# Which queue stores the last gradients of the caches: SyncE in place of GpSimd for the final 14 stores, two of them cut in 120 and 8 rows

## The chip, the core and the metric

The kernel runs on one core of a Trainium2 chip. The metric is device time in microseconds, the median of several executions; the profile shows one execution, with its own span. Engines are called TensorE (PE), VectorE (DVE), ScalarE (ACT), GpSimd (POOL) and SyncE (SP). SyncE does no arithmetic here; it issues transfers.

## What is computed

One decode step of a transformer block and its gradients. Forward: layer norm, attention of one query per batch entry over a cache of 4096 keys, output projection, residual, layer norm, a two-layer ReLU network, residual. There are 2 batch entries and 32 heads, so 64 pairs (b, h), each with a key tile and a value tile of 4096 x 128 in bf16 (1 MB). Cut to what matters:

```
q      = layernorm(x) @ wq                       # per head 128 wide
p      = softmax(q k^T / sqrt(128))              # 4096 weights per (b, h)
o      = p v ;  h = x + o @ wo ;  out_0 = h + mlp(layernorm(h))
given grad_out, go = gradient of o:
gV     = p   (outer) go                          # 4096 x 128, out_3
dp     = v go^T ;  gs = p * (dp - p.dp) / sqrt(128)
gK     = gs  (outer) q                           # 4096 x 128, out_2
```

and the gradients of x, wq, wo, w1 and w2. What has to be moved is large beside what has to be computed: all keys once, the values nearly twice (they don't stay on the chip until the gradient is known), and 128 MB of gK and gV back.

## The kernel before

**Two passes.** The first pass (`p1_iter`, index i) loads the K and V tile of a pair, computes scores, softmax and output. The second (`p2_iter`, index j, one call per turn, 64 turns) needs the gradient go of the pair; it takes the value tile Wt (kept from the first pass for 11 pairs, loaded again for 53), transposes it on TensorE in four groups (`pair_transpose`, line 439), multiplies with go (`pair_matvec`, line 452) to get dp, and makes the two outer products. `outer_half` (line 834) makes half of one on VectorE, so four such instructions per turn. gV of turn j is made in turn j; gK of turn j is made at the start of the call for turn j+1, since it needs all of dp. GpSimd copies p into a doubled form pp for gV (line 863).

**Order.** The order of every engine's instructions is written out by hand: the generators of both passes are advanced in turn, and between their steps small jobs from background lists are put in (`bg`, `bg2`, `bg3`: the network in the middle, the weight gradients in `fin_gen`, the gradient of x in `gx_gen`). Each engine then works through its list in that order, and waits where data or buffers aren't there.

**Buffers.** Tiles of 1 MB come from a set of 21 buffers that `take` and `give` hand round, first given first taken, with a tag for each use: "ld" for loads, "g" for gK and gV, "f" for weight gradients, "q" for rows of wq. `share` sets how many of each there are. In the last third of the second pass these are 6, 7, 3 and 5. A buffer given back after a store can be written again only when the store has landed, which the framework enforces with a semaphore.

**Loads.** `queue` is a plain list, filled before the kernel's main loop with all loads of K, V, W and most weights in order. `pump`, called between the steps, issues from its head as long as a buffer "ld" is free, always on SyncE (`load_tile`, line 460). The list is walked while the program is being written out, so that it is empty is known at each store then. Rows of wq for the gradient of x are loaded apart from it (line 980).

**Stores.** gK (line 872) and gV (line 891) are issued from GpSimd. Weight gradients are issued from ScalarE (line 946). The small rows, out_0 and the gradient of x, go through `store_row`, which transposes a column of 5 x 128 values, copies it and stores it from SyncE (line 655). The store of a cache gradient has 128 partitions with 8 KB each:

```
def natural(cache, b, h):
    return cache[b, h].rearrange("(p sc) d -> p sc d", sc=NSC)
```

Of the kernel before, what the change touches and what calls it, by code (L numbers as in the profile page):

```python
# [15 lines left out]
def kernel(  # L16
# [20 lines left out]
    nc = tc.nc  # L37
# [35 lines left out]
    def pst(shape, dtype, role, name):  # L73

        k = banks[role].pop(0)
        banks[role].append(k)
        return ps.tile(shape, dtype, tag=f"bank{k}", bufs=1, name=name)
# [11 lines left out]
    def take(tag, shape, name):  # L89
        assert free[tag] > 0, (tag, name)  # L90
        free[tag] -= 1
        k = homes[tag].pop(0)
        t = pools[k].tile(shape, BF16, tag=f"big{k}", bufs=1, name=name)
        home_of[id(t)] = (tag, k, t)
        return t
# [9 lines left out]
    def give(t, to=None):  # L105
        tag, k, _ = home_of.pop(id(t))
        to = to or goes_to(tag)
        owned[tag] -= 1
        owned[to] += 1
        free[to] += 1  # L110
        homes[to].append(k)
        given_at[k] = step[0]
# [280 lines left out]
    NP1 = len(pairs)  # L393
# [37 lines left out]
    def pair_transpose(nat, g, dve=False, busy=0):  # L431


        t_ps = pst([128, GT // 2, 128], FP32, "tps", "t_ps")
        warm(t_ps[:].rearrange("p j k -> p (j k)"), nat, g, busy)
        natf = nat[:].bitcast(FP32)
        for j in range(GT // 2):
            cc = (g * GT) // 2 + j
            nc.tensor.transpose(t_ps[:, j, :], natf[:, 2 * cc:2 * cc + 2, :].rearrange("p c k -> p (c k)"), ident_f[:])  # L439
        t_sb = mats.tile([128, GT // 2, 128], FP32, tag="XT", bufs=5, name="t_sb")  # L440
        if dve:
            nc.vector.tensor_copy(out=t_sb[:], in_=t_ps[:])
        else:
            nc.scalar.copy(out=t_sb[:], in_=t_ps[:])  # L444
        return t_sb

    def pair_matvec(dst, t_sb, g, vecs):
        v = t_sb[:].bitcast(BF16).rearrange("p j (k two) -> p j k two", two=2)
        for j in range(GT // 2):
            sc = g * GT + 2 * j  # L450
            for par in range(2):
                nc.tensor.matmul(dst[:, sc:sc + 2], lhsT=v[:, j, :, par], rhs=vecs[:, par, :],  # L452
                                 start=(par == 0), stop=(par == 1))

    def natural(cache, b, h):
        return cache[b, h].rearrange("(p sc) d -> p sc d", sc=NSC)
# [192 lines left out]
    def store_row(col_bf, n, dst):  # L649

        t = pst([16, 128], BF16, "mid", "row_ps")
        nc.tensor.transpose(t[0:n, :], col_bf, ident_bf[:])
        r = small.tile([16, 128], BF16, tag="orow", bufs=2, name="orow")
        nc.vector.tensor_copy(out=r[0:n, :], in_=t[0:n, :])
        nc.sync.dma_start(out=dst, in_=r[0:n, :])

    def ttr(in0, in1, acc, width, kc=128, junk=None):
        if junk is None:
# [48 lines left out]
    def mlp_out():  # L707

        ml32 = small.tile([128, ND, B], FP32, tag="ml32", bufs=1, name="ml32")
        nc.vector.memset(ml32[:], 0.0)  # L710
        for k in range(NW2):
            while free["q"] < 1:
                yield
            t = load_w2(k, "q", "(p c) d -> p c d")
            yield from wait(12)
            c1 = min(NF, (k + 1) * FP)
            m_ps = pst([128, ND, B], FP32, "mid", "mlp_ps")
            for c in range(ND):
                for cf in range(k * FP, c1):
                    kc = f_kc(cf)  # L720
                    nc.tensor.matmul(m_ps[:, c, :], lhsT=t[0:kc, cf - k * FP, c * 128:(c + 1) * 128],
                                     rhs=arow[0:kc, cf, :], start=(cf == k * FP), stop=(cf == c1 - 1))
            give(t)
            yield
            nc.vector.tensor_tensor(out=ml32[:], in0=m_ps[:], in1=ml32[:], op=ALU.add)
        ml_bf = small.tile([128, ND, B], BF16, tag="ml_bf", bufs=1, name="ml_bf")
        nc.vector.tensor_copy(out=ml_bf[:], in_=ml32[:])
        y_bf = small.tile([128, B, ND], BF16, tag="y_bf", bufs=1, name="y_bf")
        nc.vector.tensor_tensor(out=y_bf[:].rearrange("p b c -> p c b"), in0=h1c[:], in1=ml_bf[:], op=ALU.add)
        yield from wait(3)  # L730
        for b in range(B):
            store_row(y_bf[:, b, :], ND, out_0[b].rearrange("s (c p) -> (s c) p", p=128))
            yield
# [98 lines left out]
    def outer_half(dst, row, colp, k):  # L832
        sl = slice(k * HALF, (k + 1) * HALF)
        nc.vector.tensor_tensor(  # L834
            out=pairs_view(dst[:, sl, :]),
            in0=row.rearrange("p (a two) -> p a two", two=2)[:, None, :, :].to_broadcast([128, HALF, 64, 2]),
            in1=colp[:, sl, None, :].to_broadcast([128, HALF, 64, 2]), op=ALU.mult)

    def p2_iter(j, busy):

        c = S2[j] if j < NP1 else None
        p = S2[j - 1] if j >= 1 else None
        if p is not None:
            bp, hp = turns[j - 1]
            pair_matvec(p["dp"], p.pop("T3"), 3, gom[:, hp, bp, :, :])
            gsp = small.tile([128, NSC, 2], BF16, tag="gsp", name="gsp")
            nc.vector.scalar_tensor_tensor(
                out=gsp[:], in0=p["dp"][:, :, None].to_broadcast([128, NSC, 2]), scalar=negdot[:, hp, bp:bp + 1],
                in1=P_bf[:, bp * H + hp, :, None].to_broadcast([128, NSC, 2]), op0=ALU.add, op1=ALU.mult)
        if c is not None:  # L850
            b, h = turns[j]
            go = gom[:, h, b, :, :]

            bank = pst([128, 512], FP32, "sps", "dp_ps")
            for k, col in enumerate((goc, qsc)):
                nc.tensor.matmul(bank[:, 128 + k * 128:256 + k * 128],  # L856
                                 lhsT=col[:, h, b:b + 1].to_broadcast([128, 128]), rhs=ident_bf[:],
                                 start=True, stop=True)
            c["dp"] = bank[:, 0:NSC]
            rb = mats.tile([128, 256], BF16, tag="rb", bufs=4, name="rb")  # L860
            nc.scalar.activation(out=rb[:], in_=bank[:, 128:384], func=ACT.Copy, scale=rt[:, b, h:h + 1])  # L861
            pp = small.tile([128, NSC, 2], BF16, tag="pp", name="pp")
            nc.gpsimd.tensor_copy(out=pp[:], in_=P_bf[:, b * H + h, :, None].to_broadcast([128, NSC, 2]))
            c.update(rb=rb, pp=pp)
            c["T0"] = pair_transpose(c["W"], 0, busy=busy)
        if p is not None:
            gK = take("g", [128, NSC, 128], "gK")
            outer_half(gK, p["rb"][:, 128:256], gsp, 0)
        yield
        if p is not None:  # L870
            outer_half(gK, p["rb"][:, 128:256], gsp, 1)
            nc.gpsimd.dma_start(out=natural(out_2, bp, hp), in_=gK[:])  # L872
            give(gK)
            del S2[j - 1]
        yield
        if c is None:
            return
        c["T1"] = pair_transpose(c["W"], 1, busy=busy)
        pair_matvec(c["dp"], c.pop("T0"), 0, go)
        yield  # L880
        c["T2"] = pair_transpose(c["W"], 2, busy=busy)
        pair_matvec(c["dp"], c.pop("T1"), 1, go)
        yield
        c["T3"] = pair_transpose(c["W"], 3, busy=busy)
        give(c["W"], "g" if j < H and j != 1 and owned["g"] < 3 else None)
        pair_matvec(c["dp"], c.pop("T2"), 2, go)
        gV = take("g", [128, NSC, 128], "gV")
        outer_half(gV, c["rb"][:, 0:128], c["pp"], 0)
        yield
        outer_half(gV, c["rb"][:, 0:128], c["pp"], 1)  # L890
        nc.gpsimd.dma_start(out=natural(out_3, b, h), in_=gV[:])  # L891
        give(gV)
        yield

# [79 lines left out]
    def gx_gen(fin):  # L974
# [47 lines left out]
        for b in range(B):  # L1022
            gxo = small.tile([128, ND], BF16, tag="gxo", bufs=2, name="gxo")
            nc.vector.tensor_copy(out=gxo[:], in_=gx_bf[:, :, b])
            yield from wait(2)
            store_row(gxo[:], ND, out_1[b].rearrange("s (c p) -> (s c) p", p=128))
            yield
# [55 lines left out]
    queue = []  # L1083
# [51 lines left out]
    for n, (i, j) in enumerate(plan):  # L1135
# [21 lines left out]
        if j is not None:  # L1157
            while g2 is not None:
                p2_step()
            if j < NP1:  # L1160
                bg_until(("go", *turns[j]))
            g2 = p2_iter(j, 0)
# [93 lines left out]
```

## Time and profile before

| | before |
|---|---|
| median of 3 runs | 910.61 us (910.49 to 913.68) |
| span of the profiled execution | 912.4 us |
| moved by DMA | 363.00 MB, mean 398 GB/s |
| read from and written to HBM | 212.16 MB and 149.13 MB |
| SyncE's queue (all loads, small rows) | 212.18 MB, 58.0% of 16 engines' span |
| GpSimd's queue (gK and gV) | 134.23 MB, 35.5% |
| ScalarE's queue (weight gradients) | 14.91 MB, 4.1% |
| median time from issue to landing, gV and gK | 15.1 and 15.3 us |
| last product of VectorE ends | 896.05 us |

The page gives the busy share of each engine over the whole span, then rows of 40 digits, one for each fortieth of the span, in which 9 means at least 90 per cent. A line of the timeline has the start, the length, the engine, the line of the kernel, the operation, what it writes and reads, and in brackets how long the engine was idle before and what ended that. A line of the windows has for each engine its busy time and number of instructions, then the clock that TensorE was granted, the share of the 16 DMA engines in use, and GB/s. The time from issue to landing counts until the slowest of the 16 engines has reported. A transfer is made of packets, here mostly of 8 KB, one for each partition; the trace has a record of each, with its queue, start and length, though not the number of its DMA engine.

### The profile page before, as it was taken

The page shows a single profiled execution, that of the slowest core. Times are in us where ns is not written, and L with a number is a line of the kernel's source. Part 1 is how long each engine was busy: PE and PEld are TensorE (multiplying, and loading weights), DVE is VectorE, ACT ScalarE, POOL GpSimd, SP SyncE. Part 2 cuts the span into 40 slices and gives each one's busy share as a digit, 9 for nine tenths or more (in the row PEclk, how much of TensorE's full clock was granted, in tenths as well). Part 3 has the DMA queues.
Part 4 walks back from the last instruction along what each step waited for, and adds up shares of the span by engine and source line. Part 5 has one row for each costly group of instructions (what it writes and reads, how often), then busy time and mean ns, then how long its engine had stood idle before and what let it go on. Part 6 is the DMA issues. An engine that isn't in the chain of part 4 may idle for free.

```text
span 912.4 us, 26504 instructions
## 1 busy us (share of the span) xinstructions
PE 739.9 (81%) x11226; PEld 619.8 (68%) x11226; DVE 693.5 (76%) x1291; ACT 530.5 (58%) x1096; POOL 174.2 (19%) x329
## 2 busy tenths in 40 slices
PE   5998899999989898897867844866799778949780
PEld 5887787888878787787757734755667566735460
DVE  4655677877779887786868798977797468999882
ACT  4565455567677776675743433644577656537650
POOL 1222223323201111010011111111232111111120
PEclk9999899999999999998995785766557555555655
DMA  9999999999789999999999999999999999999995
GB/s 346 416 396 411 405 393 410 412 418 375 296 315 334 413 422 421 421 424 418 420 400 391 414 425 412 395 402 389 390 403 390 425 424 426 423 424 424 421 421 247
DMA packets 59479, 363.00 MB, mean 398 GB/s; under 512 B 5697, under 2 KB 15553, under 8 KB 19169
## 3 DMA queue, kind: packets, MB, share of 16 engines
q1 hardware_dynamic: 37920, 212.18, 58.0%
q0 software_dynamic: 18432, 134.23, 35.5%
q10 hardware_dynamic: 3008, 14.91, 4.1%
q8 instruction: 88, 1.44, 0.6%
q14 instruction: 31, 0.25, 0.1%
HBM read 212.16 MB, written 149.13 MB: 396 GB/s over the span
## 4 chain that ended last, share of the span: by engine, by line
PE 38%; DMA 26%; DVE 18%; ACT 10%; issue 6%; POOL 1%; SPq 0%; POOLq 0%; ACTq 0%; DVEq 0%
DMA Vt<-in_A_v_cache_dram 12%; PE t_ps L439 8%; PE m_ps L473 8%; PE t_ps L418 7%; DMA out_dram<-gV 6%; DVE gV L834 5%; DMA out_dram<-gK 5%; ACT t_sb L423 4%; DVE gK L834 3%; PE s_ps L429 3%; ACT t_sb L444 3%; DMA wqs<-in_A_wq_dram 3%; DVE pk L480 3%; DVE junk L660 2%; PE u_ps L502 2%
## 5 line engine op out<-in xcount | busy, mean ns | idle before, releaser
L423 ACT COPY t_sb<-t_ps 128x1024 bf16<-128x1024 bf16 x223 | 217.4, 1017 | 45.1 <-PE t_ps L418 44.8
L444 ACT COPY t_sb<-t_ps 128x512 f32<-128x512 f32 x256 | 149.7, 588 | 131.7 <-PE t_ps L439 128.5
L480 DVE TENSOR_TENSOR pk<-Kt,ep 128x2048 bf16<-128x2048 bf16 x128 | 156.2, 1221 | 55.8 <-ACT ep L528 25.6
L439 PE MATMUL t_ps<-ident_f,Wt 128*128 128x128 f32 x848 | 190.7, 370 | 2.1 <-ACT t_sb L423 2.1
L473 PE MATMUL m_ps<-pk,Vt 128*128 128x129 bf16 x2048 | 172.0, 222 | 16.2 <-DMA Vt<-in_A_v_cache_dram 14.8
L834 DVE TENSOR_TENSOR gK<-rb,gsp 128x2048 bf16<-128x2048 bf16 x128 | 152.5, 1225 | 29.1 <-DMA out_dram<-gV 27.1
L834 DVE TENSOR_TENSOR gV<-rb,pp 128x2048 bf16<-128x2048 bf16 x128 | 152.9, 1218 | 18.4 <-DMA out_dram<-gK 16.3
L418 PE MATMUL t_ps<-ident_bf,Kt 128*128 128x128 bf16 x2048 | 153.1, 224 | 8.6 <-DMA Kt<-in_A_k_cache_dram 3.4
L473 PEld LDWEIGHTS <-Vt 128*128 128x128 bf16 x2048 | 125.4, 99 | 46.7 <-issue 30.0
L439 PEld LDWEIGHTS t_ps<-ident_f,Wt 128*128 128x128 f32 x848 | 131.6, 192 | 35.9 <-issue 28.1
L418 PEld LDWEIGHTS <-Kt 128*128 128x128 bf16 x2048 | 125.6, 100 | 16.2 <-issue 9.1
L452 PEld LDWEIGHTS <-t_sb 128*128 128x128 bf16 x2048 | 95.5, 106 | 44.2 <-issue 18.9
L490 POOL COPY pk<-ep 128x16 bf16<-128x16 bf16 x80 | 66.4, 833 | 189.0 <-ACT ep L528 154.5
L452 PE MATMUL dp_ps<-gom,t_sb 128*128 128x2 bf16 x2048 | 95.0, 167 | 8.9 <-ACT t_sb L444 7.8
L429 PE MATMUL s_ps<-qc,t_sb 128*128 128x1 bf16 x2048 | 88.0, 164 | 1.6 <-DVE t_sb L421 0.8
L891 POOL DMA_DIRECT2D out_dram<-gV x64 | 34.3, 535 | 272.0 <-DVE gV L834 195.0
L872 POOL DMA_DIRECT2D out_dram<-gK x64 | 34.1, 533 | 260.5 <-DVE gK L834 202.0
L429 PEld LDWEIGHTS <-t_sb 128*128 128x128 bf16 x2048 | 77.6, 97 | 4.2 <-ACT t_sb L423 1.2
L944 ACT CAST ot<-o_ps 128x512 bf16<-128x512 f32 (+4 forms) x160 | 70.2, 489 | 17.3 <-DMA out_dram<-ot 11.5
L861 ACT ACTIVATE rb<-dp_ps,rt 128x256 bf16<-128x256 f32 x64 | 30.4, 475 | 60.2 <-PE dp_ps L856 58.9
L587 ACT CAST MT<-m_ps 128x128 bf16<-128x128 f32 x64 | 17.1, 267 | 75.0 <-PE m_ps L473 74.9
L660 DVE CUSTOM_DVE_ANT_0 junk<-wo_t,hbc 128x640 bf16<-128x640 bf16 x64 | 52.3, 817 | 0.2
(194 smaller groups left out, 777.9 us busy)
## 6 DMA issues: line engine op xcount, KB each, us to landing
Kt<-in_A_k_cache_dram SPq DMA_DIRECT2D x64, 1024.0 KB, 14.7
Vt<-in_A_v_cache_dram SPq DMA_DIRECT2D x64, 1024.0 KB, 15.7
out_dram<-gV POOLq DMA_DIRECT2D x64, 1024.0 KB, 15.1
out_dram<-gK POOLq DMA_DIRECT2D x64, 1024.0 KB, 15.3
Wt<-in_A_v_cache_dram SPq DMA_DIRECT2D x53, 1024.0 KB, 12.0
wo_t<-in_A_wo_dram SPq DMA_DIRECT2D x4, 1280.0 KB, 19.4
wqs<-in_A_wq_dram SPq DMA_DIRECT2D x5, 1024.0 KB, 19.8
wq_t<-in_A_wq_dram SPq DMA_DIRECT2D x5, 960.0 KB, 14.7
```

Source lines behind the costliest of these rows:

```text
L418: nc.tensor.transpose(t_ps[:, j, :], nat[:, g * GT + j, :], ident_bf[:])
L423: nc.scalar.copy(out=t_sb[:], in_=t_ps[:])
L429: nc.tensor.matmul(dst[:, sc:sc + 1], lhsT=t_sb[:, j, :], rhs=vec, start=True, stop=True)
L439: nc.tensor.transpose(t_ps[:, j, :], natf[:, 2 * cc:2 * cc + 2, :].rearrange("p c k -> p (c k)"), ident_f[:])
L444: nc.scalar.copy(out=t_sb[:], in_=t_ps[:])
L452: nc.tensor.matmul(dst[:, sc:sc + 2], lhsT=v[:, j, :, par], rhs=vecs[:, par, :], start=(par == 0), stop=(par == 1))
L473: nc.tensor.matmul(r["m"][:, 0:129], lhsT=r["V"][:, sc, :], rhs=r["pk"][sc // HALF][:, sc % HALF, 0:129], start=(sc == 0), stop=(sc == NSC ...
L480: nc.vector.tensor_tensor(out=p["pk"][k][:, :, 0:128].rearrange("p s (a two) -> p s a two", two=2), in0=p["K"][:, sl, :].rearrange("p s (a ...
L490: nc.gpsimd.tensor_copy(out=col, in_=e)
L660: nc.vector.tensor_tensor_reduce(out=junk[0:kc, 0:width], in0=in0, in1=in1, scale=1.0, scalar=0.0, op0=ALU.mult, op1=ALU.add, accum_out=acc)
L834: nc.vector.tensor_tensor(out=pairs_view(dst[:, sl, :]), in0=row.rearrange("p (a two) -> p a two", two=2)[:, None, :, :].to_broadcast([128 ...
L944: nc.scalar.copy(out=ot[0:P, k, n0:n0 + nn], in_=o_ps[0:P, 0:nn])
```

## The change

While loads are still to be issued, gK and gV are stored from GpSimd as before. Once the list of loads is empty, SyncE has nothing to issue, and its queue takes the stores of gK and gV. Two of the last three stores of gK (turns 61 and 62) are cut in two transfers, of the first 120 partitions and of the last 8. The purpose is to use the queue that has become free, and to spread the last transfers otherwise over the DMA engines. The stores of small rows leave SyncE's queue for GpSimd's, so that they don't stand between loads and stores there. What is computed is the same.

```
     def store_row(col_bf, n, dst):
...
-        nc.sync.dma_start(out=dst, in_=r[0:n, :])
+        nc.gpsimd.dma_start(out=dst, in_=r[0:n, :])
...
+    def store_tile(dst, t, uneven=False):
+
+        eng = nc.gpsimd if queue else nc.sync
+        if uneven:
+            eng.dma_start(out=dst[0:120], in_=t[0:120])
+            eng.dma_start(out=dst[120:128], in_=t[120:128])
+        else:
+            eng.dma_start(out=dst, in_=t[:])
...
-            nc.gpsimd.dma_start(out=natural(out_2, bp, hp), in_=gK[:])
+            store_tile(natural(out_2, bp, hp), gK, NP1 - 3 <= j - 1 < NP1 - 1)
...
-        nc.gpsimd.dma_start(out=natural(out_3, b, h), in_=gV[:])
+        store_tile(natural(out_3, b, h), gV)
```

## The prediction

> **What bounds the kernel now.** I read the page first. Turn j is one (b, h) of the second pass; V57 is the store of gV of turn 57, K57 that of gK. From the page:
>
> ```profile
> PE 739.9 (81%) x11226; PEld 619.8 (68%) x11226; DVE 693.5 (76%) x1291; ACT 530.5 (58%) x1096; POOL 174.2 (19%) x329
> DMA  9999999999789999999999999999999999999995
> out_dram<-gV POOLq DMA_DIRECT2D x64, 1024.0 KB, 15.1
> out_dram<-gK POOLq DMA_DIRECT2D x64, 1024.0 KB, 15.3
> ```
>
> No engine is full, but the DMA row is: the transfers bound the kernel up to its last slice, where the digit falls to 5. The change acts there, so next I cut the end into windows (last columns: clock, DMA share, GB/s).
>
> ```profile
> 898.00:900.00 2.00, 0.00 (x0) 0.00 (x0) 0.00 (x0) 0.00 (x0) 0.00 (x0) 0.50 1.02 426
> 901.00:902.00 1.00, 0.00 (x0) 0.00 (x0) 0.00 (x0) 0.00 (x0) 0.00 (x0) 0.50 0.76 320
> 902.00:904.00 2.00, 0.00 (x0) 0.00 (x0) 0.00 (x0) 0.00 (x0) 0.00 (x0) 0.50 0.37 156
> 904.00:906.00 2.00, 0.00 (x0) 0.00 (x0) 0.00 (x0) 0.00 (x0) 0.00 (x0) 0.50 0.17 74
> 908.00:910.00 2.00, 0.00 (x0) 0.00 (x0) 0.00 (x0) 0.00 (x0) 0.00 (x0) 0.50 0.07 29
> ```
>
> All compute is over at 896, and the share is full until 901. Then it falls to 0.17 (under three of 16 engines) and 0.07 (one). So one DMA engine works alone from about 906 to 910. The packet records agree: 11 engines end between 901.2 and 902.7, two at 904.0, then 905.7, 906.1, and one at 910.26. That laggard is never idle at the end: it takes a row of 8 KB each 0.306 us, eight to a store, 2.45 us, and the last stores land 2.45 us apart (905.81, 908.24, 910.66). The span ends 1.73 us after the last landing.
>
> The third view is VectorE's timeline before that:
>
> ```profile
> 854.06 1.22 DVE L834 TENSOR_TENSOR gK<-rb,gsp 128x2048 bf16<-128x2048 bf16 x1 [2.78 <-DMA out_dram<-gV]
> 858.88 1.23 DVE L834 TENSOR_TENSOR gV<-rb,pp 128x2048 bf16<-128x2048 bf16 x1 [0.17 <-DMA out_dram<-gK]
> 877.02 0.28 DVE L847 SCALAR_TENSOR_TENSOR gsp<-dp_ps,negdot,P_bf 128x64 bf16<-128x64 f32 x1 [2.04 <-PE dp_ps L452]
> 893.69 2.36 DVE L834 TENSOR_TENSOR gK<-rb,gsp 128x2048 bf16<-128x2048 bf16 x2
> ```
>
> gV and gK rotate through seven buffers here (share gives g=5+2), so an outer product waits for the landing seven stores earlier: K57 at 854.06 waits for V54, issued 823.01, landed 853.97. These waits total 3 us and are nearly absent later, but with little to spare (below). Last, GpSimd's queue:
>
> ```profile
> 893.75 0.53 POOL L891 DMA_DIRECT2D out_dram<-gV  x1 [1.92 <-DVE gsp L847]
> 896.34 0.53 POOL L872 DMA_DIRECT2D out_dram<-gK  x1 [2.06 <-DVE gK L834]
> ```
>
> K63 is computed by 896.05, issued 0.29 us later, and the earliest engine takes its first row at 898.25, 1.9 us after issue.
>
> [...]from 843 to 857 a busy engine takes in turn one row of GpSimd's queue, one of SyncE's, one (4 KB) of ScalarE's. [...]The two x loads of 10 rows show 10 packets each[...]; the records don't number engines. [...]Here it is 0.96 us (x load issued 0.75, first packet 1.71) against 1.9. The laggard takes none of the five packets of the second 5-row store[...].
>
> **Which stores move.** The list empties when turn 63's Wt load is issued. Six buffers hold Wt, so that load follows turn 57's last transposes, between the halves of gV. In the trace it is issued at 846.10, V57 at 850.25. From V57 on all moves: 7 gV and 7 gK, 14 of 128; K61 and K62 in two parts, so 16 issues on SyncE.
>
> **Part 1, the split.** [...]16 x 0.306 = 4.9 us.[...] Alone, a gain of 3.6 to 4.2 us.
>
> **Part 2, shorter issue.** Issue after VectorE: 0.03 us for SyncE's small store against 0.29. Start: 0.96 against 1.9. Together K63's first row can come 1.2 us earlier after compute. Today this is worth nothing on the laggard, which has 10 us queued when K63 is issued; it counts only if compute sets the end. Behind the waiting stores on SyncE nothing is queued: no load is left (last wqs load 815.08). On GpSimd pp no longer stands behind a store's wait; VectorE is not waiting for pp there, so nothing.
>
> **Part 3, the small rows.** Four stores of 1.2 KB move to GpSimd, 0.53 us each, in idle time. Behind them wait pp copies, of 0.25 to 0.41 us; also nothing. Taking the first two off SyncE frees a Wt load from a wait of at most 4.5 us, in a saturated stretch: nothing.
>
> **Part 4, two queues in place of one.** This is the cost. At 857.2 the last Wt row has passed and GpSimd's queue holds K54 (nearly done), V55, K55, V56, K56. They land now at 858.76, 861.30, 864.31, 868.18, 871.39, with V57 behind them. After the change SyncE's queue has V57 (and K57, V58, ...) ready, and they go row for row with the old ones. Each old store is stretched by up to its own 2.45 us:
>
> K54 +1.0, lands 859.8. V55 +3.5, 864.8. K55 +6.0, 870.3. V56 +8.4, 876.6. K56 +10.9, 882.3.
>
> The newer ones get ahead, but VectorE needs the buffers in the old order. K58 (now 863.76) needs V55: +1.0. V59 (866.57) needs K55: +3.7. K59 (870.26) needs V56: +6.3. V60 (872.54) needs K56: +9.8. From K60 on the needed stores are all SyncE's and long landed. So VectorE is 9.8 us late at V60; the bounds are 8 (SyncE's queue runs dry at times) and 12 (the waits feed back into V57's neighbours, another queue takes turns). It regains its later waits for TensorE (2.04 + 0.69 + 0.36 = 3.1 us), since TensorE can work up to two banks ahead meanwhile. K63 is then computed 6.7 us late, at 902.8 (bounds 901 to 905).
>
> **The sum.** Queues are by then nearly empty, so K63 lands 0.03 + 0.96 + 2.45 + 0.45 (last row to landing, as now) = 3.9 us later: 906.7, or 904.9 to 908.9. The laggard's own limit, if relieved, is 905.4 + 0.45; the second engine's 906.5 to 907.1. The later counts: 906.5 to 908.9, against 910.66. The gain is 1.8 to 4.2 us; I take 2.8, towards the late side of the wait, as part of the 9.8 feeds back. 910.6 - 2.8 = 907.8.
>
> **Rivals.** (A) The old stores aren't held up (the queues are served by age, or buffers are free sooner): only the balance counts, gain 4.2, or 5 if the second engine also catches up: 905.6 to 906.4. For: waits are nearly absent today. Against: strict alternation in the packets. (B) The laggard isn't relieved[...]: its work is unchanged or 0.6 us more: 910.6 to 911.2. For: no numbers in the records. (C) Slower: the delay reaches 12 to 15 us and TensorE gives nothing back, at a clock of 0.5: K63 computed at 908 to 911, landed at 912 to 915, total 911.9 to 915.5. For: every buffer waits on the slowest of 16 engines. Against: while VectorE waits, SyncE's queue drains and the old stores get the whole engine.
>
> **How the numbers follow.** Main case 0.50, A 0.23, B 0.17, C 0.10. The range 905.4 to 911.8 leaves out most of C and a little of A. Half a per cent is 4.55 us: faster needs under 906.06, which is most of A and a sliver of the main case, 0.22. Slower needs over 915.2, the end of C with some unknown: 0.07. Same: 0.71.
>
> **What would show it.** Timeline of VectorE, 860 to 885: several idle times ended by the landing of a store, about 10 us in all, where before there are none; without them A is right. Windows after 900: the share falls without a lone engine of 4 us; if 0.07 stands for 4 us again, B. K63's product ending near 903 and its landing 4 us later show the sum. 57 stores of each kind left on GpSimd. What would make it wrong: a different engine lagging after the change, or the wait for buffers moving to earlier turns.

## The result, and the profile after

| | before | after |
|---|---|---|
| median | 911.67 us (910.49 to 913.68, 4 runs) | 919.58 us (918.83 to 921.13, 4 runs) |
| ratio | | 1.0087, 95% interval 1.0062 to 1.0112 |
| span of the profiled execution | 912.4 us | 916.8 us |
| last product of VectorE ends | 896.05 us | 903.48 us |
| last packet of a store ends | 910.26 us | 915.1 us |

The kernel became slower by about 0.9%. The prediction, 907.8 us with a range up to 911.8, missed on the side to which it had given 7 in 100. The medians lie 7.9 us apart, the two profiled executions only 4.4 us in span (the profiled one of before took 914.32 us, longer than its four timed runs; that of after, 918.83 us, is the shortest of its four). What is read from the profiles below bears on the 4.4 us; the rest isn't traced. From the page of the kernel after, the DMA row, the row of GB/s, and the three groups of stores that take the place of the two shown of before:

```profile
DMA  9999999999889999999999999999999999999987
GB/s 346 419 394 411 407 395 409 413 418 368 310 287 349 421 422 423 422 422 422 411 410 388 408 425 413 398 408 391 392 404 386 425 424 424 421 425 422 424 338 244
out_dram<-gV POOLq DMA_DIRECT2D x57, 1024.0 KB, 13.3
out_dram<-gK POOLq DMA_DIRECT2D x57, 1024.0 KB, 13.8
out_dram<-gV SPq DMA_DIRECT2D x7, 1024.0 KB, 10.7
```

57 stores of each kind stay on GpSimd, as counted. Read the last two columns of the first two rows together. The last but one slice is 80 to 89% busy and moves 338 GB/s; a slice with 9 moves 424. The last digit is higher than before (7 against 5), which on its own would look like the better balance that the change is for.

The windows of the kernel after, in stretches of 2 us (last three columns: clock, DMA share, GB/s):

```profile
892.00:894.00 2.00, 2.00 (x21) 1.88 (x19) 2.00 (x4) 1.17 (x2) 1.08 (x2) 0.50 1.07 439
896.00:898.00 2.00, 2.00 (x17) 1.72 (x16) 1.97 (x4) 1.23 (x3) 0.13 (x1) 0.50 0.94 254
898.00:900.00 2.00, 1.56 (x23) 1.36 (x21) 2.00 (x3) 1.11 (x2) 0.00 (x0) 0.75 1.06 262
902.00:904.00 2.00, 0.00 (x0) 0.00 (x0) 1.48 (x2) 0.00 (x0) 0.00 (x0) 0.61 0.96 307
908.00:910.00 2.00, 0.00 (x0) 0.00 (x0) 0.00 (x0) 0.00 (x0) 0.00 (x0) 0.50 0.97 385
912.00:914.00 2.00, 0.00 (x0) 0.00 (x0) 0.00 (x0) 0.00 (x0) 0.00 (x0) 0.50 0.09 37
```

This is the reading of the case. From 898 to 900 before, a share of 1.02 moved 426 GB/s. Now a share of 1.06 moves 262. The engines are as busy and move 0.6 of the bytes, so the rows take longer. The packet records give it: up to 894.6 nearly all rows of 8 KB take 0.31 us; from 894.64, when the first 120-row part begins to be moved, rows of about 0.6 us appear, and in the 4 us from 896 the mean is 0.507 us.

VectorE's timeline after shows the waits for buffers, and the last product:

```profile
859.60 1.23 DVE L834 TENSOR_TENSOR gV<-rb,pp 128x2048 bf16<-128x2048 bf16 x1 [1.32 <-DMA out_dram<-gK]
871.17 2.36 DVE L834 TENSOR_TENSOR gV<-rb,pp 128x2048 bf16<-128x2048 bf16 x2 [3.58 <-DMA out_dram<-gK]
877.38 2.36 DVE L834 TENSOR_TENSOR gK<-rb,gsp 128x2048 bf16<-128x2048 bf16 x2 [2.57 <-DMA out_dram<-gV]
883.57 2.36 DVE L834 TENSOR_TENSOR gV<-rb,pp 128x2048 bf16<-128x2048 bf16 x2 [3.82 <-DMA out_dram<-gK]
901.12 2.36 DVE L834 TENSOR_TENSOR gK<-rb,gsp 128x2048 bf16<-128x2048 bf16 x2
```

The line at 883.57 is V60, 11.0 us late; in the kernel before it has no wait:

```profile
872.54 2.35 DVE L834 TENSOR_TENSOR gV<-rb,pp 128x2048 bf16<-128x2048 bf16 x2
```

And SyncE's instructions, where line 843 issues a part of 120 rows, 844 one of 8 rows, and 846 a whole store:

```profile
893.78 0.35 SPq L843 DMA_DIRECT2D out_dram<-gK  x1
894.19 0.31 SPq L844 DMA_DIRECT2D out_dram<-gK  x1
896.05 0.36 SPq L846 DMA_DIRECT2D out_dram<-gV  x1
898.64 0.38 SPq L843 DMA_DIRECT2D out_dram<-gK  x1
899.07 1.60 SPq L844 DMA_DIRECT2D out_dram<-gK  x1
900.91 2.63 SPq L846 DMA_DIRECT2D out_dram<-gV  x1
903.64 2.06 SPq L846 DMA_DIRECT2D out_dram<-gK  x1
```

K61's large part takes 7.1 us to land, then V62 9.3, K62's large part 11.5 and V63 12.1 us. The time to landing grows with each of them.

### The profile page after: what moved, and what is told of

The parts are those of the page before. It is cut to its first block, busy times and chain, and to the rows that moved or that the text cites. A ratio compares the mean times of both kernels' runs of the same rounds, so it can differ in the third digit from the quotient of the medians.

```text
span 916.8 us, 26507 instructions
## 1 busy us (share of the span) xinstructions
PE 747.8 (82%) x11226; PEld 626.5 (68%) x11226; DVE 693.5 (76%) x1291; ACT 531.0 (58%) x1096; POOL 169.0 (18%) x319
## 4 chain that ended last, share of the span: by engine, by line
PE 39%; DMA 26%; DVE 19%; ACT 9%; issue 6%; DVEq 0%; SPq 0%; POOL 0%; ACTq 0%; POOLq 0%
DMA Vt<-in_A_v_cache_dram 12%; PE t_ps L439 8%; PE m_ps L473 8%; PE t_ps L418 7%; DMA out_dram<-gK 7%; DVE gV L834 5%; DMA out_dram<-gV 4%; DVE gK L834 4%; ACT t_sb L423 4%; PE s_ps L429 3%; PE u_ps L502 3%; DMA wqs<-in_A_wq_dram 2%; DVE junk L660 2%; PE o_ps L947 2%; DVE pk L480 2%
## 5 line engine op out<-in xcount | busy, mean ns | idle before, releaser
L439 PE MATMUL t_ps<-ident_f,Wt 128*128 128x128 f32 x848 | 197.4, 380 | 1.4 <-ACT t_sb L423 1.4
L439 PEld LDWEIGHTS t_ps<-ident_f,Wt 128*128 128x128 f32 x848 | 136.1, 197 | 35.1 <-issue 28.5
L490 POOL COPY pk<-ep 128x16 bf16<-128x16 bf16 x80 | 62.8, 786 | 192.2 <-ACT ep L528 158.1
L846 POOL DMA_DIRECT2D out_dram<-gV x57 | 30.6, 536 | 254.4 <-DVE gV L834 201.3
L846 POOL DMA_DIRECT2D out_dram<-gK x57 | 30.4, 534 | 240.7 <-DVE gK L834 191.0
```

Source lines behind the costliest of these rows:

```text
L490: nc.gpsimd.tensor_copy(out=col, in_=e)
```

## The experiments

Each ratio is to the kernel before, with its 95% interval. Letters stand for theories: P, the rows of transfers with fewer partitions are themselves slow; U, the uneven share of the two parts is what costs; Q, the additional issues on SyncE cost; L, the engine that lags at the end does so because GpSimd's queue stored, and M, against it, that it lags whatever the queue.

**No split.** The kernel after with K61 and K62 stored whole.

```
-            store_tile(natural(out_2, bp, hp), gK, NP1 - 3 <= j - 1 < NP1 - 1)
+            store_tile(natural(out_2, bp, hp), gK)
```

> The change without its split: K61 and K62 go in one transfer of 128 rows each from SyncE. Theory P (the rows of the split transfers are slow, 0.6 us in place of 0.31[...]): rows at the end take 0.31 us again, VectorE still computes K63 at about 903.5, it lands some 4 us later, near 907.5, and the time is 2 to 4 us below the kernel before. Theory Q (SyncE as issuer of stores is what is slow at the end, with issues of up to 2.6 us): the stores still land 10 us or more after their issue, and the time stays 5 to 9 us above the kernel before.

Measured: ratio 0.9993 (0.9977 to 1.0010), span 911.7. The whole loss is gone, and with it the long rows, though VectorE still waits for buffers. The gain of 2 to 4 us that was expected did not come. From VectorE's timeline of this kernel:

```profile
870.48 2.36 DVE L834 TENSOR_TENSOR gV<-rb,pp 128x2048 bf16<-128x2048 bf16 x2 [1.90 <-DMA out_dram<-gK]
876.71 2.36 DVE L834 TENSOR_TENSOR gK<-rb,gsp 128x2048 bf16<-128x2048 bf16 x2 [2.59 <-DMA out_dram<-gV]
882.33 2.36 DVE L834 TENSOR_TENSOR gV<-rb,pp 128x2048 bf16<-128x2048 bf16 x2 [3.26 <-DMA out_dram<-gK]
899.88 2.36 DVE L834 TENSOR_TENSOR gK<-rb,gsp 128x2048 bf16<-128x2048 bf16 x2
```

K63 is computed at 902.24, 6.2 us later than before, and issued at 902.26; 14 engines end by 906.08, 3.8 us after the issue. One more ends at 907.7, and one goes on, as its windows show:

```profile
904.00:906.00 2.00, 0.00 (x0) 0.00 (x0) 0.00 (x0) 0.00 (x0) 0.00 (x0) 0.50 0.96 401
906.00:908.00 2.00, 0.00 (x0) 0.00 (x0) 0.00 (x0) 0.00 (x0) 0.00 (x0) 0.50 0.11 45
908.00:910.00 2.00, 0.00 (x0) 0.00 (x0) 0.00 (x0) 0.00 (x0) 0.00 (x0) 0.50 0.07 29
```

A share of 0.07, one engine of 16, stands until 910.25, where it stood before (910.26).

**Halves of 64 rows.** The kernel after with its split parts in equal halves.

```
-            eng.dma_start(out=dst[0:120], in_=t[0:120])
-            eng.dma_start(out=dst[120:128], in_=t[120:128])
+            eng.dma_start(out=dst[0:64], in_=t[0:64])
+            eng.dma_start(out=dst[64:128], in_=t[64:128])
```

> The change with K61 and K62 cut in 64 and 64 rows in place of 120 and 8[...]. Theory P: [...]rows take about 0.6 us here too, and the time is 5 to 9 us above the kernel before, like the change. Rival U (the cost is the uneven share, 15 engines and then 8): rows take 0.31 us and the time is that of the version with no split, below the kernel before.

Measured: ratio 1.0049 (1.0025 to 1.0072). In the kernel before, a load of 64 partitions (issued at 105.99) has 16 landings, as many as there are engines. If the halves are shared out like it, which no record shows, every engine has four rows of each, and it costs all the same. So the loss doesn't need an uneven share, and U falls as its cause; that the share adds something (0.49% here, 0.87% in the change) isn't excluded. Its windows in the same stretch:

```profile
896.00:898.00 2.00, 1.70 (x25) 1.46 (x24) 1.97 (x3) 1.55 (x3) 1.15 (x1) 1.00 1.05 221
898.00:900.00 2.00, 1.46 (x29) 1.05 (x27) 2.00 (x3) 1.17 (x2) 0.00 (x0) 1.00 0.90 213
```

Busy, and at half the bytes.

**Halves of the columns.** The kernel after with two transfers again, but each with all 128 partitions and 4 KB of each.

```
-            eng.dma_start(out=dst[0:120], in_=t[0:120])
-            eng.dma_start(out=dst[120:128], in_=t[120:128])
+            eng.dma_start(out=dst[:, 0:HALF], in_=t[:, 0:HALF])
+            eng.dma_start(out=dst[:, HALF:], in_=t[:, HALF:])
```

> The change with K61 and K62 cut along the row in place of across partitions: two transfers of 128 partitions and 4 KB each, so the number of issues is the change's[...]. Theory P: packets of 4 KB take 0.16 us, nothing is slow, and the time is within 1 us of the version with no split. Theory Q (more issues on SyncE): like the change, 5 to 9 us above the kernel before.

Measured: ratio 1.0001 (0.9981 to 1.0022). Most packets of 4 KB take 0.16 us, half of 0.31. It issues as often on SyncE as the change does, and nothing is lost: Q falls. What costs in these versions is a transfer that takes fewer than 128 partitions.

**The split alone.** The kernel before, with K61 and K62 in 120 and 8 rows from GpSimd, all else as before.

```
-            nc.gpsimd.dma_start(out=natural(out_2, bp, hp), in_=gK[:])
+            if NP1 - 3 <= j - 1 < NP1 - 1:
+                nc.gpsimd.dma_start(out=natural(out_2, bp, hp)[0:120], in_=gK[0:120])
+                nc.gpsimd.dma_start(out=natural(out_2, bp, hp)[120:128], in_=gK[120:128])
+            else:
+                nc.gpsimd.dma_start(out=natural(out_2, bp, hp), in_=gK[:])
```

> The kernel before with the split alone, K61 and K62 in 120 and 8 rows, all from GpSimd as before. Theory P: VectorE's times are those of the kernel before (K63 computed near 896), the packets of K61 and K62 take about 0.6 us, about 5 us more for most engines, so the end comes 0 to 3 us later than before. The prediction's step (the split frees the last engine of 4.9 us and costs 0.6): 3 to 4 us faster than before.

Measured: ratio 1.0048 (1.0027 to 1.0069). SyncE issues no store, and the long rows are there. VectorE computes K63 at 898.4, 2.3 us later than before, but was as late well ahead of the split (K57 at 856.39 against 854.06), so the split isn't what delays it. Its windows:

```profile
892.00:894.00 2.00, 1.75 (x32) 1.41 (x30) 1.88 (x3) 1.40 (x3) 0.62 (x2) 1.00 1.00 295
900.00:902.00 2.00, 0.00 (x0) 0.00 (x0) 0.00 (x0) 0.00 (x0) 0.00 (x0) 0.50 0.91 254
912.00:914.00 2.00, 0.00 (x0) 0.00 (x0) 0.00 (x0) 0.00 (x0) 0.00 (x0) 0.50 0.13 53
```

K63, issued at 898.91, lands at 917.11, 6.5 us later than before (910.66). With the 2.3 us taken off, that is 4.2 us; the expectation had 0 to 3.

**Six split stores in place of two**, turns 57 to 62, in the kernel before: `if NP1 - 7 <= j - 1 < NP1 - 1`, the rest as in the split alone.

> The kernel before with six stores of gK (turns 57 to 62) split in 120 and 8 rows in place of two, all from GpSimd. If each split store costs the engines up to 2.45 us by rows of double length, and the two cost 0.48 per cent (4.4 us) together, six cost 9 to 14 us. If the cost comes only from the two stores at the very end (order of the last transfers), six cost no more than two, 3 to 6 us.

Measured: ratio 1.0138 (1.0103 to 1.0172). That is 1.38% against 0.48%, 2.9 times the loss for three times the split stores (the intervals are 1.03 to 1.72% and 0.27 to 0.69%), as P has it. The rows of 8 KB on the two queues of the stores, from 870 us to the end, tell the same (counts are of the rows on record; lengths between the classes are left out; the last column adds up what each takes over 0.309 us and divides by 16 engines):

```
kernel                 rows  0.28-0.34 us  0.55-0.70 us  1 us and more  excess / 16
before                 1493          1447             1              0      0.4 us
no split               1483          1443             2              0      0.7
halves of the columns  1155          1109             1              0      0.5
change                 1453          1222            85              7      3.9
split alone            1566          1325           100              7      4.3
halves of 64 rows      1585          1327           139             27      5.6
six split              1522          1092           163             30      7.7
```

**More buffers.** No split, and the buffers that held Wt go to the front of the set for gK and gV once the list of loads is empty.

```
-        give(c["W"], "g" if j < H and j != 1 and owned["g"] < 3 else None)
+        if queue:
+            give(c["W"], "g" if j < H and j != 1 and owned["g"] < 3 else None)
+        else:
+            give(c["W"], "g")
+            homes["g"].insert(0, homes["g"].pop())
```

> The version with no split, in which the six Wt buffers go to gK and gV, first in line, as soon as all loads are issued. Prediction's part 4 (VectorE waits for the old stores' buffers because SyncE's new stores share the engines with them): these waits vanish, and K63 is computed near 896 as in the kernel before, in place of 902 to 903. If the end is set by the laggard's own work, as the version with no split suggests (K63 lands 8.4 us after its issue there), the time is that of the version with no split within 1 us in spite of that. Rival (the end is paced by VectorE): 4 to 6 us faster.

Measured: ratio 0.9996 (0.9980 to 1.0012). From VectorE's timeline, its only wait for a store after 850, and its last product:

```profile
854.10 1.23 DVE L834 TENSOR_TENSOR gK<-rb,gsp 128x2048 bf16<-128x2048 bf16 x1 [2.24 <-DMA out_dram<-gV]
893.56 2.36 DVE L834 TENSOR_TENSOR gK<-rb,gsp 128x2048 bf16<-128x2048 bf16 x2
```

K63 is issued at 895.95, 6.3 us earlier than without the additional buffers, and lands at 910.28 against 910.70. VectorE's waits are real and cost nothing; the lagging engine sets the end either way.

**Small rows alone.** The kernel before with `nc.gpsimd.dma_start(out=dst, in_=r[0:n, :])` in line 655.

> The kernel before with the small rows alone moved to GpSimd's queue. Prediction's part 3: no change, within 1 us. Rival: GpSimd waits for the rows with pp copies behind it, so gV comes later, 1 to 3 us slower.

Measured: ratio 1.0002 (0.9988 to 1.0016): nothing.

**Which engine lags.** In the first two attempts (three kernels), an additional transfer within HBM is meant to load some of the engines and not the others, so that the end moves if the laggard is among them. That it falls on some engines alone is the author's estimate. The first adds 8 x 8 rows to the kernel without the split, ahead of V57; eight rows of 0.306 us on the laggard would move the end by 2.45 us. Its expectation has first the outcome for a laggard among the loaded engines, then that for one that isn't.

```
+        if not queue and not extra:
+            scratch = nc.dram_tensor("extra_rows", (8, 8, 4096), BF16).ap()
+            src = A_k_cache[0, 0].rearrange("(p r c) d -> p r (c d)", p=8, r=16)[:, 0:8, :]
+            nc.sync.dma_start(out=scratch, in_=src)
...
```

> The version with no split, with one more transfer ahead of V57 on SyncE: 8 x 8 rows of 8 KB from the key cache to a scratch buffer in HBM that nothing reads[...]. It asks which engine comes last.[...] all its later landings and the end come about 2.45 us later than in the version with no split.[...] the other engines have over 2.5 us of slack and the end stays within 0.7 us.

Measured: ratio 1.0036 (1.0017 to 1.0056), 0.43% or 3.9 us more than without the rows, as if the laggard were among the loaded ones. The transfer had 8 packets of 65,536 B, eight rows each. But the profile ends only 0.8 us later (911.09), with 13 engines that end by 909.46. The two don't agree on the size, so this doesn't tell who lags. The next two put 8 x 16 rows, and 7 x 16 rows, into the kernel with more buffers; sixteen rows on the laggard would be 4.9 us. The outcomes expected of the first stand in the same order; of the second they are those for a laggard loaded by 8 x 16 rows alone, by both, and by neither.

> The version with no split and with more buffers (in which VectorE waits for no store after 857), with one transfer of 8 x 16 rows of 8 KB from HBM to an unread scratch buffer ahead of V57[...] it has no slack and the end comes about 4.9 us later than without the rows.[...] the others' slack (the next ends 4.3 us before it) absorbs it, and the end is at most 1 us later.

> The same with 7 x 16 rows[...] this costs at most 1 us[...].[...] both cost 4.9.[...] neither costs more than 1 us.

Measured: 1.0016 (1.0000 to 1.0032) and 1.0010 (0.9993 to 1.0027). Both missed their aim: the trace shows 16 packets of 65,536 B in one and 16 of 57,344 B in the other. The transfer, contiguous on both sides, was cut in 16 equal packets in both, as many as there are engines, so nothing shows that an engine was left out. Nothing follows on the laggard.

The third attempt puts marks ahead of K63 in the kernel without the split: six small transfers of 5, 6, 7, 8, 14 and 15 rows, each with its own row length, so that every packet can be told.

```
+            if j - 1 == NP1 - 1:
+                for k, w in ((5, 192), (6, 320), (7, 256), (8, 512), (14, 768), (15, 1024)):
+                    mark = nc.dram_tensor(f"mark{k}", (k, 4096), BF16).ap()
+                    src = A_k_cache[0, 0].rearrange("(p c) d -> p (c d)", p=128)
+                    nc.sync.dma_start(out=mark[:, 0:w], in_=src[0:k, 0:w])
```

> The version with no split, with six small transfers ahead of K63 on SyncE, from the key cache to unread scratch in HBM, of 5, 6, 7, 8, 14 and 15 rows with a row length of its own each (384, 640, 512, 1024, 1536 and 2048 bytes), so that a packet tells by its size to which transfer it belongs. [...]The time itself asks nothing.

Measured: 912.11 us, with 913.85 of the kernel before beside it, one run each. Each mark has as many packets as rows. All but one of each start between 901.2 and 904.1. The last ones follow each other without a gap, as on one engine:

```
start us   length of row   mark
905.77        384 B        5 rows
905.80        640 B        6 rows
905.83        512 B        7 rows
905.86       1024 B        8 rows
905.91       1536 B        14 rows
905.97       2048 B        15 rows
906.06       8192 B        K63, eight rows to 908.67; the other engines end by 907.36
```

So the laggard takes part in all six, that of 5 rows too: none of them leaves it out. Which engine it is isn't shown, as the records have k packets for k rows, not the engines' numbers. And the marks tell this of one execution without the split, in which the laggard ends 1.3 us after the others; that the same engine lags in the kernel before is taken over, not shown.

**Stores without GpSimd.** In three versions of the kernel before, the stores made while the share of "g" is 5 and more, 51 of the 64 of each kind and the first of them at about 478 us, go to another engine's queue: to ScalarE and issued a step or more later, to SyncE likewise, and to SyncE at once. The core of the first two, with `nc.scalar` or `nc.sync`:

```
+    def store_late(dst, t):
+        if owned["g"] < 5:
+            nc.gpsimd.dma_start(out=dst, in_=t[:])
+            give(t)
+        else:
+            late_stores.append((dst, t, now[0]))
...
+        while late_stores and late_stores[0][2] < j:
+            one_late()
```

> The kernel before, in which gK and gV are stored from ScalarE, one or two steps after they are made, as soon as five buffers are theirs (the pure second pass, some 47 turns); GpSimd keeps the earlier ones. Theory L (one DMA engine falls behind because of GpSimd's queue): the last stores land within 1 us on all engines, no engine works alone at the end, and the end comes 4 to 6 us earlier relative to VectorE's last product. Theory M (it falls behind whatever the queue): the tail of one engine stays, and the time is that of before or longer by what the waits on ScalarE cost.

> As the version with stores from ScalarE, but from SyncE: in the pure second pass each gV and gK is issued from SyncE one or two steps after it is made, in one order with the loads, and no tile is split. Theory L (the one engine falls behind because of GpSimd's queue): the engines end within 2 us of one another, as they did with ScalarE; VectorE is not held by ScalarE's waits, so the time is 2 to 5 us below the kernel before. Rival (loads stand behind stores that wait for VectorE): loads come late, VectorE's last product comes after 900, and the time is above the kernel before.

> As the run before it, but each store is issued from SyncE at the place where the kernel before has it, without delay. Theory L: engines end together, as there. Waits of SyncE for VectorE are longer than in the delayed form, so the time is between that of the delayed form and 8 us above it.

Measured: ratios 1.0103 (1.0072 to 1.0133), 1.0204 (1.0149 to 1.0259) and 1.0155 (1.0109 to 1.0201). All lose, and the expectation of a gain on SyncE was wrong. K63 is computed late, its product starting at 907.59 on SyncE with delay and at 913.87 without, against 893.69 before. But on SyncE the engines are still full up to 922 and 926, 12 and 10 us after that product has ended, so it isn't what sets the end there; they moved too little earlier. From 700 to 800 us they moved 367 and 383 GB/s on SyncE, with and without delay, and 395 with ScalarE, against 424 before. In the first two no engine is left alone for long. From the windows of the delayed SyncE version:

```profile
920.00:922.00 2.00, 0.00 (x0) 0.00 (x0) 0.00 (x0) 0.00 (x0) 0.00 (x0) 0.50 1.00 422
922.00:924.00 2.00, 0.00 (x0) 0.00 (x0) 0.00 (x0) 0.00 (x0) 0.00 (x0) 0.50 0.45 188
924.00:926.00 2.00, 0.00 (x0) 0.00 (x0) 0.00 (x0) 0.00 (x0) 0.00 (x0) 0.50 0.02 4
```

The engines end within 1.8 us of each other (922.3 to 924.1), and with ScalarE within 1.8 us. That fits L. The third doesn't: with the stores issued at once from SyncE, the engines end between 926.8 and 930.4, 3.6 us apart, and the last works alone for 1.4 us, where the expectation had them end together. A rival to L also stands untested: in all three the engines had stretches in which they weren't full (a DMA share of 0.88 to 0.94 over 50 us and more, against 0.99 to 1.01 before), and a lagging engine may have caught up there. L isn't shown.

## Why the prediction was wrong, point by point

**Part 1, the split: the step that failed, in both of its terms.** The prediction valued the split at 3.6 to 4.2 us, as if it took sixteen rows of 0.306 us, 4.9 us, off the lagging engine. That the split would spare this engine was a guess, as its words "the records don't number engines" concede. First, the engine is not spared. In the trace of the change a whole store has 16 landings, a part of 120 rows 15 and a part of 8 rows 8 (beside one event at the issue of each part), so not every engine has a share in a part. But K62's parts have their last landings at 910.18 and 910.57, 2.9 and 2.4 us after the ones before, and then come V63 at 913.02 and K63 at 915.45, each another 2.4 us on, as eight rows take. So, as these times follow each other, the engine that ends last has rows of both parts. If 120 rows on 15 engines are eight each, and 8 rows on 8 engines one each, it takes nine rows of a split store in place of eight: two rows more in all if K61 is like K62, and no relief. The nine are an estimate from the numbers of landings, and K61's parts (last landings 900.88 and 901.38, 0.2 and 0.4 us after the ones before) don't set one engine apart. The marks agree: without the split the laggard takes part in all six small transfers, that of 5 rows too. The prediction had read from the packets that the laggard "takes none of the five packets" of a 5-row store. The marks speak against that reading: packets of equal length, which carry no engine's number, were probably strung together to the wrong engine. Rival B, the laggard not relieved, had 0.17; without the split, its picture of a laggard with its old work is what the chip shows (0.9993).

Second, the prediction priced the rows of the parts at 0.306 us as all others. In the change, rows of 0.55 to 0.70 us and some of over 1 us appear as soon as a part of 120 rows is moved. Whether other stores in flight are slowed too isn't shown, as a row can't be told to its store. Five runs show that it is the parts with fewer partitions that do this: gone when the stores are whole or cut in columns, there with 64 and 64 rows, there from GpSimd's queue too, and about three times the loss with six. By the table the long rows cost 3.5 us over before, spread on 16 engines. The end of the change, 915.1, lies 4.8 us behind that of before: the 3.5, and the two rows more of the laggard (the estimate above), which at 0.3 to 0.6 us each come to 0.6 to 1.2, would make 4.1 to 4.7. This is an estimate from those numbers: the 3.5 are a mean of 16 engines, and how much of it fell on the laggard is not known. In the split alone the long rows come to 3.9 us over before, beside the 4.2 us found there.

Why the rows grow isn't shown: no record tells which engine moved a row. In the run with halves their lengths gather at about 0.3, 0.6 and 1.18 us, once, twice and four times the row of a whole store.

**Part 2, the shorter issue:** worth nothing, as said, but not of the size said. (The prediction's 0.96 and 1.9 us are the times from issue to first packet, of SyncE's x load and of GpSimd's K63.) SyncE's issues took 0.31 to 0.38 us up to 898.64, with at most three earlier stores or parts of its queue still to land, and 1.60, 2.63 and 2.06 us for the last three, with four. Without the split all 14 issues took 0.33 to 0.35 us.

**Part 3, the small rows:** nothing, as said (1.0002).

**Part 4, two queues side by side:** right, within 1.2 us for each store. K54, V55, K55, V56 and K56 landed at 859.47, 864.63, 871.04, 877.29 and 883.44, where 859.8, 864.8, 870.3, 876.6 and 882.3 were worked out. V60 was 11.0 us late (9.8, bounds 8 to 12), and K63 was computed at 903.5 (902.8). Its cost was misplaced: 14 engines ended 3.8 us after K63's issue in the run without the split, where the sum had 3.9 us to landing, and it was not the end. The run with more buffers takes the waits away and ends at the same time.

**The sum and the rivals.** The sum let compute set the end because Part 1 had taken the laggard out of it. Rival C was on the right side for another reason: its delay of 12 to 15 us in K63 did not come (7.4 us). No case held that rows themselves would grow longer; the range was built from waits and balance alone, and each price of a row was taken from rows of whole stores. Two of the sum's figures are slightly off, without effect: the last row ends 0.40 us ahead of the landing (910.26 to 910.66), not 0.45, and a landing at 915 puts the end of C at 914.9, not 915.5.

**Left open.** The change loses 0.87%, the split alone 0.48%, and the intervals overlap a little; their profiled spans stand the other way round (916.8 and 918.9). That in the change the slow rows fall on a queue that compute feeds late, with nothing else to fill the engines, would explain a difference, but no run tells this apart. And no version tried beats the kernel before: the four closest to it (no split, cut in columns, more buffers, small rows alone) all hold 1 in their interval.

## What to carry to other kernels

Price a transfer by a row of the same shape: what a part with fewer partitions takes per row (about 0.6 us here) can't be read from whole tiles (0.31 us). In windows, read GB/s beside the DMA share, as full engines that move 0.6 of the bytes (262 GB/s at a share of 1.06, 426 at 1.02) are a loss that no row of busy time shows. And before a transfer is cut to take work off a lagging engine, find out whether it spares that one: the landings of its parts show it (here the last one comes 2.9 and 2.4 us after the others), and transfers of different row lengths and numbers of rows just ahead of the end leave marks in the packet records that tell in which of them it takes part.

## What the runs showed of the hardware

- A row of 8 KB took 0.31 us in a store of 128 partitions, and about 0.6 us, at times 1.2 us, when stores of 120 and 8 or of 64 and 64 partitions were in flight. Two halves by columns kept 0.16 us for 4 KB.
- The issue of a store on SyncE took 0.33 to 0.35 us in the version without the split and up to 2.63 us in the change. Parts aren't needed for a longer one: with whole stores alone, in the delayed SyncE version, it took up to 1.39 us where several followed each other closely (900.75). Six marks took 5.22 us together.
- A contiguous copy within HBM was cut in 16 packets whether its outer size was 8 or 7 (65,536 and 57,344 B); with 8 of the 16 rows taken from each of 8 blocks it had 8 packets of 65,536 B.
- In the kernel before, and in the versions without the split, cut in columns and with more buffers, one engine ended 4 to 8 us after most of the others (910.26 against 902.7 in the kernel before). In the two that gave 51 of the 64 stores of each kind, delayed, to ScalarE or SyncE it was 1.8 us from the first to the last, in the one that gave them to SyncE at once 3.6 us.
